# Transposed query features, sums as extra columns and no max subtraction in a gated linear-attention kernel

## Chip, cores and metric

One core of one Trainium2 chip. The metric is the device time of the core, in microseconds. A run counts as slow when it lies over 1.5% above the fastest run of the same kernel.

## The reference, cut to what matters

```python
qkv = (x @ wqkv)            # x: 2048 x 1024 bf16; 32 heads of 32
pq = einsum("bhsd,hdf->bhsf", q, w_phi);  pk = the same of k
phi_q = concat([softmax(pq), softmax(-pq)], -1)      # 64 features a head
phi_k = concat([softmax(pk), softmax(-pk)], -1)
kv = einsum("bhsf,bhsd->bhfd", phi_k, v);  z = phi_k summed over s
o  = (phi_q @ kv) / (phi_q . z + 1e-6)
a  = o @ wo
# b: x, plus a gated FFN (3584 wide) on the one row with the largest x . w_r
# out = g * a + (1 - g) * b,  g = sigmoid(x . gate_w), one value a row
```

All sums over k must be complete before the first q row can be finished. So the kernel has a K half (V, k features, kv) and a Q half (q features, numerator, wo), and the FFN of one row is spread among them as filler.

## The kernel before

The k and q features fold w_phi into wqkv first (`wkf`, `wqf`). A half tile is 128 rows by 16 heads. The softmax runs in stages that the loop spreads over several rounds, and TensorE (PE) transposes the finished q features (`eT`) before the numerator. Cuts are marked.

```python
def softmax_front(p_ps):                       # stage 0: copy of the scores
    nc.scalar.copy(out=ps_[:], in_=p_ps[:])
def softmax_mm(st, d2_pool):                   # stage 1: max, min, two subtractions
    nc.vector.tensor_reduce(out=mx[:], in_=st["ps"][:], axis=AX.X, op=ALU.max)
    nc.vector.tensor_reduce(out=mn[:], in_=st["ps"][:], axis=AX.X, op=ALU.min)
    nc.gpsimd.tensor_tensor(out=d1[:], in0=st["ps"][:], in1=_bc(mx[:], ...), op=ALU.subtract)
    # d2: the same with mn, on POOL for q, on DVE for k
def softmax_exp(st):                           # stage 2
    nc.scalar.activation(out=e[:, :, 0, :], in_=st["d1"][:], func=ACTF.Exp)
    nc.scalar.activation(out=e[:, :, 1, :], in_=st["d2"][:], func=ACTF.Exp, scale=-1.0)
def softmax_norm(st, normalize):               # stage 3: DVE sums; POOL scales
    ...
def q_s4(u):                                   # PE transposes of e, copied by ACT
    for pl in range(NPU):
        nc.tensor.transpose(out=eT_ps[:, pl, :], in_=e[...], identity=ident[:])
    nc.scalar.copy(out=eT[:], in_=eT_ps[:])
def q_s5(u):                                   # numerator (64 columns), denominator (2 columns)
    ...
def q_s6(t):                                   # PE transposes of o, copied by ACT
    ...
# weights: loaded plainly, transposed on PE; logits: 128 matmuls of 2 columns on PE
```

## Time and profile before

| | before |
|---|---|
| median | 356.94 us (356.36 to 357.41, 4 runs) |
| mean granted clock of PE | 0.992 |
| PE busy | 318.7 us, 89% of the span |
| PE idle, 40 to 220 us | 17.6 us (180 less 162.4) |

The page also divides the span into 40 slices. A digit is the busy share of a slice in tenths; `PEclk` is PE's granted clock in tenths of full speed (9 is 90% or more). This is PE in the kernel before:

```profile
PE   2998996989989899698989898999999999999982
PEclk9999999989999999999999999999999999999998
```

PE falls short of 9 in many slices up to slice 25 (223 us; the last kv matmul of the K half starts at 196.5) and is full from there to the tail.

### The profile page before, as it was taken

How to read it: one execution, taken by the hardware profiler on the slowest of the kernel's cores; microseconds unless marked ns; L12 is line 12 of the kernel's file. 1: busy time of each engine (PE TensorE's matmuls, PEld its weight loads, DVE VectorE, ACT ScalarE, POOL GpSimd, SP SyncE). 2: the span in 40 equal slices, each digit the busy share in tenths (PEclk: the TensorE clock that was granted, in tenths of full speed). 3: DMA queues.
4: the chain of work that ended last, by engine and by line, in shares of the span. 5: the costliest groups of instructions: out<-in, count | busy, mean ns of one | idle time of the engine just before them, and what ended most of it. 6: DMA issues, size and time to landing. Idle time of an engine off the chain costs nothing. (4 is left out here: it accounts for less than half of the span.)

```text
span 356.3 us, 8221 instructions
## 1 busy us (share of the span) xinstructions
PE 318.7 (89%) x3322; PEld 189.1 (53%) x3372; DVE 258.5 (73%) x455; ACT 211.8 (59%) x333; POOL 202.8 (57%) x231
## 2 busy tenths in 40 slices
PE   2998996989989899698989898999999999999982
PEld 1578552445555555354446475555555555556640
DVE  3034288877987975688887989888888888887641
ACT  1456645535556655254554679777777777778630
POOL 1000056467776763577778978687777766665101
PEclk9999999989999999999999999999999999999998
DMA  8997920028823033333336660012221111122111
GB/s 253 375 386 238 324 87 2 0 87 272 261 94 118 2 120 118 120 118 120 120 118 237 233 245 31 31 59 61 61 60 61 60 60 46 59 61 62 47 59 30
DMA packets 33894, 43.60 MB, mean 122 GB/s; under 512 B 2624, under 2 KB 23104, under 8 KB 33856
## 3 DMA queue, kind: packets, MB, share of 16 engines
q1 hardware_dynamic: 32704, 43.00, 35.5%
q8 instruction: 26, 0.43, 0.5%
q10 hardware_dynamic: 1120, 0.07, 0.2%
q14 instruction: 12, 0.10, 0.1%
q0 software_dynamic: 32, 0.00, 0.0%
HBM read 38.87 MB, written 4.20 MB: 121 GB/s over the span
## 5 line engine op out<-in xcount | busy, mean ns | idle before, releaser
L247 POOL TENSOR_TENSOR d<-pks,mx 128x512 bf16<-128x512 bf16 x64 | 67.1, 1049 | 89.1 <-DVE mx L243 82.4
L263 DVE TENSOR_REDUCE ssum<-e 128x32 f32<-128x1024 bf16 x64 | 77.4, 1211 | 33.3 <-ACT e L257 33.2
L256 ACT ACTIVATE e<-d 128x512 bf16<-128x512 bf16 x64 | 40.5, 633 | 61.7 <-POOL d L247 55.4
L269 POOL TENSOR_TENSOR phi<-e,rs 128x1024 bf16<-128x1024 bf16 x32 | 61.2, 1912 | 22.0 <-DVE rs L267 21.0
L304 PE MATMUL pk<-wkf,xT 128*128 128x512 bf16 x242 | 61.7, 385 | 4.6 <-DVE d L251 4.1
L352 PE MATMUL pq<-wqf,xT 128*128 128x512 bf16 x237 | 59.2, 379 | 3.9 <-ACT pks L235 2.0
L292 PE MATMUL pv<-wv_sb,xT 128*128 128x512 bf16 x248 | 61.1, 385 | 0.8 <-issue 0.2
L428 PE MATMUL kv_b<-wo_sb,oT 128*128 128x512 bf16 x247 | 57.1, 379 | 1.5 <-ACT oT L416 1.0
L243 DVE TENSOR_REDUCE mx<-pks 128x16 f32<-128x512 bf16 x64 | 42.4, 662 | 17.2 <-ACT pks L235 13.9
L257 ACT ACTIVATE e<-d 128x512 bf16<-128x512 bf16 x64 | 40.4, 631 | 7.6 <-POOL d L249 7.2
L374 ACT COPY eT<-eT_ps 128x1024 bf16<-128x1024 bf16 x32 | 32.6, 1019 | 17.6 <-PE eT_ps L370 17.6
L244 DVE TENSOR_REDUCE mn<-pks 128x16 f32<-128x512 bf16 x64 | 42.8, 669 | 0.0
L428 PEld LDWEIGHTS <-oT 128*128 128x128 bf16 x256 | 24.8, 98 | 30.2 <-ACT oT L416 1.1
L304 PEld LDWEIGHTS <-xT 128*128 128x128 bf16 x256 | 24.2, 98 | 30.2 <-issue 5.9
L292 PEld LDWEIGHTS <-xT 128*128 128x128 bf16 x256 | 24.1, 99 | 27.3 <-issue 3.1
L352 PEld LDWEIGHTS <-xT 128*128 128x128 bf16 x256 | 24.1, 97 | 27.0 <-issue 2.7
L277 POOL TENSOR_TENSOR e<-e,rho 128x512 bf16<-128x512 bf16 x32 | 33.6, 1051 | 2.5
L249 POOL TENSOR_TENSOR d<-pks,mn 128x512 bf16<-128x512 bf16 x32 | 33.6, 1049 | 1.4
L431 DVE SCALAR_TENSOR_TENSOR o_out<-kv_b,gate,xg 128x512 bf16<-128x512 f32 x32 | 23.8, 744 | 10.6 <-PE kv_b L428 7.9
L141 DVE COPY wT<-pTw 128x1024 bf16<-128x1024 bf16 x16 | 10.9, 683 | 19.7 <-PE pTw L139 19.7
L296 ACT CAST vaug<-pv 128x512 bf16<-128x512 f32 x32 | 18.6, 581 | 8.5 <-PE pv L292 8.4
L235 ACT CAST pks<-pk 128x512 bf16<-128x512 f32 x32 | 18.5, 578 | 5.7 <-PE pk L304 4.7
(94 smaller groups left out, 432.9 us busy)
## 6 DMA issues: line engine op xcount, KB each, us to landing
wch<-in_B_w_gate_dram SPq DMA_DIRECT2D x7, 1024.0 KB, 6.0
wch<-in_B_w_up_dram SPq DMA_DIRECT2D x7, 1024.0 KB, 5.1
wchd<-in_B_w_down_dram SPq DMA_DIRECT2D x7, 1024.0 KB, 5.2
xs_t<-in_A_x_dram SPq DMA_DIRECT2D x16, 256.0 KB, 5.5
xin<-in_A_x_dram SPq DMA_DIRECT2D x16, 256.0 KB, 2.7
out_dram<-o_out SPq DMA_DIRECT2D x32, 128.0 KB, 1.7
wv_sb<-in_A_wqkv_dram SPq DMA_DIRECT2D x2, 1024.0 KB, 5.7
wk_raw<-in_A_wqkv_dram SPq DMA_DIRECT2D x1, 2048.0 KB, 10.1
```

Of the source, the lines that this page charges most:

```text
L243: nc.vector.tensor_reduce(out=mx[:], in_=st["ps"][:], axis=AX.X, op=ALU.max)
L244: nc.vector.tensor_reduce(out=mn[:], in_=st["ps"][:], axis=AX.X, op=ALU.min)
L247: nc.gpsimd.tensor_tensor(out=d1[:], in0=st["ps"][:], in1=_bc(mx[:], [P, HH, DH]), op=ALU.subtract)
L249: nc.gpsimd.tensor_tensor(out=d2[:], in0=st["ps"][:], in1=_bc(mn[:], [P, HH, DH]), op=ALU.subtract)
L256: nc.scalar.activation(out=e[:, :, 0, :], in_=st["d1"][:], func=ACTF.Exp)
L257: nc.scalar.activation(out=e[:, :, 1, :], in_=st["d2"][:], func=ACTF.Exp, scale=-1.0)
L263: nc.vector.tensor_reduce(out=ssum[:].rearrange("p h s -> p (h s)"), in_=e[:].rearrange("p h s f -> p (h s) f"), axis=AX.X, op=ALU.add)
L269: nc.gpsimd.tensor_tensor(out=phi[:].rearrange("p h s f -> p (h s) f"), in0=e[:].rearrange("p h s f -> p (h s) f"), in1=_bc(rs[:].rearrang ...
L292: nc.tensor.matmul(pvf, lhsT=xT[:, kb, t * P:(t + 1) * P], rhs=wv_sb[:, kb, hf * 512:(hf + 1) * 512], start=(kb == 0), stop=(kb == KB - 1))
L304: nc.tensor.matmul(pkf, lhsT=xT[:, kb, t * P:(t + 1) * P], rhs=wkf[:, kb, hf * 512:(hf + 1) * 512], start=(kb == 0), stop=(kb == KB - 1))
L352: nc.tensor.matmul(pqf, lhsT=xT[:, kb, t * P:(t + 1) * P], rhs=wqf[:, kb, hf * 512:(hf + 1) * 512], start=(kb == 0), stop=(kb == KB - 1))
L428: nc.tensor.matmul(kv_b[nh][:], lhsT=oT[:, kb, :], rhs=wo_sb[:, kb, sl], start=(kb == 0), stop=(kb == KB - 1))
```

## The change

The intent is to take work off PE and POOL. Without max subtraction both exponentials come straight from PSUM. The q features are computed transposed (`wqf` is the stationary side), so the `eT` transposes go. The four softmax sums become eight extra columns of the numerator matmul. Weights and o are transposed by DMA. As exponentials without max subtraction can overflow, norms of x and of the folded weights bound the scores; a flag at the end selects a slow general path, never taken with these inputs. The core of the diff, shortened and with cuts:

```diff
-    nc.scalar.copy(out=ps_[:], in_=p_ps[:])          # and max, min, d1, d2
+    nc.scalar.activation(out=e[:, :, 0, :], in_=pk[:], func=ACTF.Exp)
+    nc.scalar.activation(out=e[:, :, 1, :], in_=pk[:], func=ACTF.Exp, scale=-1.0)
 ...
-    wrgT ...: 128 logit matmuls of 2 columns
+    for c in range(2):      # logits: row-sum products on DVE, two rows broadcast to 128 partitions
+        nc.vector.scalar_tensor_tensor(out=junk2[:], in0=xt_[:], scalar=1.0, in1=wr_bc[:, c, :],
+                                       op0=ALU.mult, op1=ALU.mult, accum_out=rg[:, c, t:t + 1])
+    nc.scalar.activation(out=junk[:], in_=xt_[:], func=ACTF.Square, accum_out=nx2[:, t:t + 1])
 ...
-    prep_j: 8 PE transposes of the weights, DVE copy, fold
+    nc.sync.dma_start_transpose(out=wT[which][:, :, kb * P:(kb + 1) * P], in_=A_wqkv[...])
+    fold: 8 matmuls, 2 DVE copies, and the norm:
+    nc.vector.scalar_tensor_tensor(out=junk3[:], in0=wf[:, kb, :], ..., accum_out=nw2[:, which, kb:kb + 1])
 ...
+def q_front(sb, j):   # q features transposed, 512 rows at a time
+    nc.tensor.matmul(pq[:], lhsT=wqf[:, kb, j * P:(j + 1) * P], rhs=xT[:, kb, sb * SB:(sb + 1) * SB], ...)
+def q_num(t, hf):
+    num = psK.tile([P, 3 * 512], F32, name="num", tag="kvn")        # one buffer of three banks
+    nc.tensor.matmul(num[:, b * NSTR:b * NSTR + KVW], lhsT=E[...], rhs=KV[:, sg, j, :], ...)   # 136 columns
+    # DVE: ds (copy of the sums), pr, den, rden, ab (two), then T = num * ab; POOL: o = T0 + T1
+def q_oT(t):
+    if t < NT - 1: nc.sync.dma_start_transpose(out=oT[:], in_=o_f)
+    else: 8 PE transposes and an ACT copy
 ...
+    nv = 12      # V halves taken as done when the K loop starts (16 are)
 ...
+    fv = nc.values_load(flag[0:1, 0:1], min_val=0, max_val=1)
+    with tc.If(fv > 0):
+        general_path(...)
```

## The prediction

> **What bounds the kernel now.** I read the page first: busy time, the 40 slices, the costliest groups. Then the windows of 20 us, then the timeline of TensorE (PE) in the last half, then the chain that ended last. The busy shares and four windows:
>
> ```profile
> PE 318.7 (89%) x3322; PEld 189.1 (53%) x3372; DVE 258.5 (73%) x455; ACT 211.8 (59%) x333; POOL 202.8 (57%) x231
> ...
> 0.00:20.00 20.00, 12.92 (x70) 7.28 (x72) 4.00 (x9) 5.66 (x7) 1.35 (x17) 1.00 0.96 322
> 60.00:80.00 20.00, 17.42 (x157) 8.57 (x159) 16.52 (x29) 8.33 (x16) 11.89 (x11) 0.94 0.12 37
> 280.00:300.00 20.00, 19.70 (x181) 11.45 (x183) 16.89 (x31) 15.31 (x22) 14.41 (x19) 1.00 0.19 65
> 340.00:357.00 17.00, 8.55 (x59) 4.09 (x57) 4.75 (x9) 2.16 (x2) 0.95 (x1) 0.91 0.14 46
> ```
>
> After start and length, a window gives PE, weight loads, DVE, ACT, POOL. From 220 to 320 us PE is full (19.7 of 20); DVE follows at 16.9. Busy PE counts overlapping latencies, so I take the cost of a matmul from start to start:
>
> ```profile
> 261.74 1.89 PE L428 MATMUL kv_b<-wo_sb,oT 128*128 128x512 bf16 x8
> 263.47 0.61 PE L370 MATMUL eT_ps<-ident,e 128*128 128x128 bf16 x8
> 263.91 0.19 PE L399 MATMUL num_ps<-kvm,eT 128*128 128x64 bf16 x1
> ...
> 264.35 0.61 PE L414 MATMUL oT_ps<-ident,o_sb 128*128 128x128 bf16 x8
> ```
>
> Eight 512-column matmuls take 263.47-261.74 = 1.73 us (0.216 each), eight 128-column transposes 0.44 (0.055), the 16 small numerator and denominator matmuls up to 264.35 another 0.44 (0.0275). In the same way the timeline gives 0.0325 for a kv matmul and 0.025 for a one-column FFN matmul. The stream of before: 1024 x 0.216 = 221.2; 768 of 128 columns x 0.055 = 42.2; 512 x 0.0275 = 14.1; kv 256 x 0.0325 = 8.3; FFN 672 x 0.025 = 16.8; logits 128 x 0.025 = 3.2. Sum 305.8 us. So 356.3 - 305.8 = 50.5 us are PE gaps: about 10 before the first V matmul, about 12 in the tail, the rest in the K half, where PE waits for the softmax that DVE, POOL and ACT hand to each other.
>
> The groups that the argument uses (busy, mean ns of one):
>
> ```profile
> L263 DVE TENSOR_REDUCE ssum<-e 128x32 f32<-128x1024 bf16 x64 | 77.4, 1211 | 33.3 <-ACT e L257 33.2
> L269 POOL TENSOR_TENSOR phi<-e,rs 128x1024 bf16<-128x1024 bf16 x32 | 61.2, 1912 | 22.0 <-DVE rs L267 21.0
> L243 DVE TENSOR_REDUCE mx<-pks 128x16 f32<-128x512 bf16 x64 | 42.4, 662 | 17.2 <-ACT pks L235 13.9
> L374 ACT COPY eT<-eT_ps 128x1024 bf16<-128x1024 bf16 x32 | 32.6, 1019 | 17.6 <-PE eT_ps L370 17.6
> L431 DVE SCALAR_TENSOR_TENSOR o_out<-kv_b,gate,xg 128x512 bf16<-128x512 f32 x32 | 23.8, 744 | 10.6 <-PE kv_b L428 7.9
> ```
>
> 512 more elements cost a DVE reduction 1211-662 = 549 ns; I use this slope for new DVE shapes.
>
> **What the Trainium skill says.** "VectorE: DVE Perf Modes", section "The perf-mode tier table": reductions, and anything with an fp32 operand in PSUM, run at one element a cycle. The trace agrees: 549 ns for 512 elements. "SBUF — State Buffer", section "Who interferes with whom": a DVE instruction with two SBUF inputs contends with a GpSimd instruction that reads SBUF, and the second is blocked whole. The change adds 48 such instructions; before has hardly any, so its trace can't show it. "DMA: Bandwidth & Descriptors", section "Latency and other measured facts": a DMA transpose with a non-contiguous middle dimension moved 261 GB/s. Before has none; its plain loads reach 375 to 386 GB/s. "Runtime: NRT & Kernel Launch", section "Instruction fetch mechanics": a taken branch to a target out of the fetched window stalls for a fetch. Before has no such branch.
>
> **The change, part by part.** On PE: the 256 transposes of e go (256 x 0.055 = -14.1), 120 of the 128 transposes of o (-6.6, now DMA), the 128 weight transposes (-7.0, now DMA), the 128 logit matmuls (-3.2, now DVE). The 256 numerator matmuls with the sums as columns have 136 columns, an estimated 0.058 each, 15.0 against 14.1 (+0.9). The order shows 288 V matmuls for 256: four halves are computed twice (32 x 0.216 = +6.9). New stream 305.8 - 23.1 = 282.7 us.
>
> POOL loses all subtractions and the rho products: phi 61.2 and 32 additions x 1.05 = 33.6, so 203 falls to about 97. ACT loses pks and eT, gains 16 squares (about 1.1 each): about 147 from 212. Both are then far from bounding.
>
> DVE loses max, min, d2 and the q sums, but gains: 32 products with row sums for logits and 16 for the norms of the folded weights, 1024 elements each, estimated 744+549 = 1.29 us, 61.9 in all; 32 PSUM copies of folded weights (about 0.67, 21.4); per half tile of q a chain of seven: five small (0.22+0.16+0.15+0.30 and a reciprocal 0.24, from small rows of the groups) and one of 1024 elements (the old o_sb of 512 took 0.68, so 0.68+0.55 = 1.23), 2.30 x 32 = 73.6. With sums and reciprocals of k (38.8+11.0), xT copies 5.5, o_out 23.8 and some 10 of rest: 246 us, against 258.5. DVE is hardly relieved, and its work moves to the start.
>
> *Start.* On DVE the copy of the first xT stands behind five of the new products, so V starts at an estimated 13.5 us (before 9.8). The x load for tile 4 stands behind eight weight transposes: 5.5 MB ahead of it, 3.5 at 380 GB/s and 2 at 261 or less, so it lands at about 22 to 26. From there to the first k sum DVE has 18 products (23.2), 16 fold copies (10.7) and 3 xT copies (2.1) = 36 us. The K loop starts at about 58 (before about 43), after some 37 us of PE stream: about 21 us of PE gap.
>
> *K loop.* PE: k 55.3, 20 V halves 34.6, kv 8.3, FFN 9.6 to 10.4, folds and xT 6.6 = 115. In its first 7 rounds DVE needs 1.55 (sum, reciprocal) + 2.58 + 0.34 = 4.5 us a round against PE 3.8: 5 to 6 us of gap. Later PE leads. Head-of-line waits on the load queue (transposes of the q weights ahead of x tiles 12 to 15): 3.
>
> *Turn to Q* (last phi, KV copies, the FFN's hidden vector): 4, partly filled by q matmuls. *Q rounds:* PE num 0.47 + q 1.73 + wo 1.73 = 3.93; DVE 0.74 + 2.30 = 3.04, so hidden; 2 of loose gaps. *Drain:* eight rounds without q have 2.2 us of PE but 3.04 of DVE: 7. *Tail:* num, chain 2.3, POOL 1.05, transposes, ACT copy 1.0, wo 3.45, o_out, then the output and the last accumulation as before:
>
> ```profile
> 346.43 3.20 PE kv_b L428 x14
> 349.65 0.76 DVE o_out L431
> 350.43 1.69 DMA out_dram<-o_out
> 352.21 0.59 issue
> ```
>
> These 6 us from o_out to the end of the span remain; I add 2 for the flag and its branch. Tail gap 12. Gaps: 21 + 6 + 3 + 4 + 2 + 7 + 12 = 55. Sum 282.7 + 55 = 338. I write 337.
>
> **Rivals.** (a) *DVE bounds the first third more than I think.* For: 246 us of DVE, 48 products that POOL's 1.9 us phi can block. Against: POOL is only half loaded. If each product in the K loop waits 1 us and the start takes 8 more, 337 becomes 350 to 358 and the gain is gone. (b) *DMA transposes are slow.* For: short runs, one queue. In a Q round, o of a tile is ready about 4.5 us after the second numerator starts, and wo of it starts at 7.86+0.47+1.73 = 10.1: a transpose may take 5.5 us from issue. Before's plain 256 KB load landed in 2.7 us, so double is still hidden; at 8 us each of 15 tiles stalls 2.5 us (+38), and the start loses 10. That would make 360 to 385. (c) *The products are cheap* (two bf16 elements a cycle, 0.7 us): DVE in the start falls by some 11 us and the K loop is PE's alone: 318 to 325. (d) *The cut softmax chain closes the K half's gaps and nothing replaces them*: near 282.7 + 35 = 318.
>
> **Range and chances.** The PE saving of 23 us is sure; the gaps may go from 50 to 35 or to 75. So 337, with 319 to 355 eight times in ten. Faster by over 2% is under 349.4: my own sum puts it 12 us inside, 0.76. Within 2% 0.15, slower than 363.7 0.09, mostly by rival (b).
>
> **What would show it.** PE busy should fall while its gaps shift to the first 60 us; matmul counts 288 V, 256 num with 136 columns and 0.058 us spacing; DVE busy near 246 with products of 1.29; POOL under 100. First k sum near 58 us; Q rounds of 3.9 to 4.0 us; DMA transposes of o under 5.5 us from issue to landing; 2 us between the last accumulation and the end that before lacks. I am wrong if DVE is busy under 215 (c), if wo waits for oT by DMA (b), or if Q rounds are over 4.3.

## The result and the profile after

The changed kernel takes 353.24 us median (352.04 to 353.82, 4 runs) against 356.94. The ratio is 0.9882, 95% interval 0.9852 to 0.9913. All ratios here are the mean time of one kernel's fast runs over that of the other's fast runs of the same rounds, so they are not quite the ratios of the quoted medians. The prediction was 337: its range held, but the gain was a fifth of the forecast.

Busy times, then PE, DVE and the clock in slices:

```profile
PE 296.9 (84%) x2478; PEld 161.0 (46%) x2518; DVE 246.1 (70%) x501; ACT 137.4 (39%) x230; POOL 115.5 (33%) x81
...
PE   1398979879779999999998999969999999847590
...
DVE  4623999999968435599994237866777777766740
...
PEclk9999999999989999999999999999999999987987
```

PE lost 21.8 us of busy time, and 4 came out at the end. DVE is full from slice 5 to slice 11 (35 to 97 us), and from slice 35 on PE is mostly at 4 to 8 tenths, with its clock down as well. Four windows, the first three as the prediction read them before:

```profile
0.00:20.00 20.00, 6.28 (x38) 4.19 (x39) 12.59 (x22) 7.69 (x11) 5.27 (x16) 1.00 0.91 239
60.00:80.00 20.00, 15.89 (x122) 8.66 (x123) 20.00 (x31) 14.89 (x26) 8.22 (x4) 1.00 0.74 158
280.00:300.00 20.00, 19.84 (x121) 10.33 (x122) 15.37 (x42) 7.72 (x12) 6.67 (x6) 1.00 0.40 99
300.00:320.00 20.00, 13.88 (x78) 6.98 (x78) 13.91 (x41) 4.53 (x5) 5.07 (x5) 0.85 0.34 86
```

Three places stand out. PE works 6.3 of the first 20 us (12.9 before). In the early K rounds DVE is busy for all 20 us and PE for 15.9. The Q rounds are full until 300 us; then come the last eight half tiles without q matmuls, the *drain*, where PE is busy 13.9 of 20 us at a clock of 0.85.

Here is PE's timeline in the drain (start, duration, line and operation, count; in brackets the idle time ahead of it and what ended it):

```profile
307.00 1.25 PE L523 MATMUL po<-wo_sb,oT 128*128 128x512 bf16 x5 [1.61 <-DMA oT<-o_sb]
308.09 0.64 PE L480 MATMUL num<-KV,E 128*128 128x136 bf16 x8
308.78 2.32 PE L523 MATMUL po<-wo_sb,oT 128*128 128x512 bf16 x10
...
311.87 0.65 PE L480 MATMUL num<-KV,E 128*128 128x136 bf16 x8 [0.62 <-DVE T L495]
316.35 0.61 PE L523 MATMUL po<-wo_sb,oT 128*128 128x512 bf16 x1 [3.83 <-DMA oT<-o_sb]
316.75 1.11 PE L480 MATMUL num<-KV,E 128*128 128x136 bf16 x8
317.66 4.38 PE L523 MATMUL po<-wo_sb,oT 128*128 128x512 bf16 x12
```

The numerator at 316.75 has to wait behind *one* wo matmul of the next tile, and that one waits 3.83 us for a DMA transpose. Its own buffer had been free since 315.33, when the product `T` of the numerator before ended; so it lost 1.4 us by standing behind that matmul. In this trace PE keeps the order in which its matmuls were laid when the kernel was built. From 317.66 twelve matmuls take 4.38 us, where 12 x 0.216 = 2.6 would do: from 316 to 320 us, around this wait, the clock is 0.50. The DVE product `T` that frees the numerator's buffer starts at 305.29, 310.59, 314.10, 319.25, 324.35, 328.45, 331.96 and 335.48, so a round takes 30.19 / 7 = 4.31 us.

At the start, these are the loads on the queue of SyncE (SP), and then what DVE does once x tile 4 has landed:

```profile
10.32 13.69 SPq L273 DMA_TRANSPOSE wT<-in_A_wqkv_dram  x8
24.19 1.90 SPq L242 DMA_DIRECT2D xs_t<-in_A_x_dram  x4
```

```profile
27.55 1.23 DVE L265 SCALAR_TENSOR_TENSOR junk<-xs_t,wr_bc 128x1024 bf16<-128x1024 bf16 x1 [7.73 <-DMA xs_t<-in_A_x_dram]
...
35.07 1.89 DVE L283 CAST wkf<-pW 128x512 bf16<-128x512 f32 x3 [4.54 <-PE pW L281]
...
64.43 1.21 DVE L409 TENSOR_REDUCE ssum<-e 128x32 f32<-128x1024 bf16 x1
```

The last line is the first k sum. DVE waits 7.73 us for x4, and then 4.54 us for the first fold of the k weights (`pW`), which stands behind V matmuls in PE's order.

In the early K rounds two engines block each other. These are the DVE timeline and then the POOL timeline, same columns:

```profile
70.04 1.16 DVE L265 SCALAR_TENSOR_TENSOR junk<-xs_t,wr_bc 128x1024 bf16<-128x1024 bf16 x1
...
71.13 2.92 DVE L265 SCALAR_TENSOR_TENSOR junk<-xs_t,wr_bc 128x1024 bf16<-128x1024 bf16 x1
...
75.11 1.21 DVE L265 SCALAR_TENSOR_TENSOR junk<-xs_t,wr_bc 128x1024 bf16<-128x1024 bf16 x1
```

```profile
70.27 2.70 POOL L413 TENSOR_TENSOR phi<-e,rs 128x1024 bf16<-128x1024 bf16 x1 [0.38 <-DVE rs L411]
```

The product takes 1.21 us alone and 2.92 beside phi, and phi takes 2.70 instead of 1.91. This bears out the Trainium skill, "SBUF — State Buffer", section "Who interferes with whom", by which a DVE instruction with two SBUF inputs contends with a GpSimd instruction that reads SBUF, and whoever comes first blocks the other: phi starts while the product of 70.04 runs and ends at 73.0, 1.9 us after that product; the product of 71.13 ends at 74.05, 1.1 us after phi. The pattern repeats every second round (DVE: 2.91 us at 80.67, 2.92 at 90.22), and the rounds alternate between 3.6 and 5.9 us.

### The profile page after: what moved, and what is told of

The parts are those of the page before. It is cut to its first block, busy times and chain, and to the rows that moved or that the text cites. A ratio compares the mean times of both kernels' runs of the same rounds, so it can differ in the third digit from the quotient of the medians.

```text
span 352.0 us, 6368 instructions
## 1 busy us (share of the span) xinstructions
PE 296.9 (84%) x2478; PEld 161.0 (46%) x2518; DVE 246.1 (70%) x501; ACT 137.4 (39%) x230; POOL 115.5 (33%) x81
## 5 line engine op out<-in xcount | busy, mean ns | idle before, releaser
L499 POOL TENSOR_TENSOR o_sb<-T 128x512 bf16<-128x512 f32 x32 | 40.6, 1267 | 108.2 <-DVE T L495 108.2
L523 PE MATMUL po<-wo_sb,oT 128*128 128x512 bf16 x249 | 63.0, 394 | 10.7 <-DMA oT<-o_sb 10.3
L459 PE MATMUL pq<-xT,wqf 128*128 128x512 bf16 x244 | 59.8, 379 | 0.9 <-ACT E L462 0.3
L265 DVE SCALAR_TENSOR_TENSOR junk<-xs_t,wr_bc 128x1024 bf16<-128x1024 bf16 x32 | 42.8, 1364 | 13.6 <-DMA xs_t<-in_A_x_dram 13.6
L409 DVE TENSOR_REDUCE ssum<-e 128x32 f32<-128x1024 bf16 x32 | 38.7, 1208 | 17.1 <-ACT e L406 17.1
L495 DVE TENSOR_TENSOR T<-num,ab 128x1024 f32<-128x1024 f32 x32 | 39.2, 1225 | 3.5 <-DVE ab L493 0.5
L393 ACT CAST v_all<-pv 128x512 bf16<-128x512 f32 x36 | 21.2, 588 | 47.5 <-PE pv L391 47.5
L391 PEld LDWEIGHTS <-xT 128*128 128x128 bf16 x288 | 27.0, 100 | 27.9 <-issue 2.2
L525 DVE SCALAR_TENSOR_TENSOR o_out<-po,gate,xg 128x512 bf16<-128x512 f32 x32 | 23.8, 745 | 22.0 <-PE po L523 22.0
L402 PEld LDWEIGHTS <-xT 128*128 128x128 bf16 x256 | 24.1, 98 | 26.5 <-issue 1.3
L459 PEld LDWEIGHTS <-wqf 128*128 128x128 bf16 x256 | 23.5, 97 | 23.5 <-issue 0.6
```

Of the source, the lines that this page charges most:

```text
L265: nc.vector.scalar_tensor_tensor(out=junk2[:], in0=xt_[:], scalar=1.0, in1=wr_bc[:, c, :], op0=ALU.mult, op1=ALU.mult, accum_out=rg[:, c, ...
L391: nc.tensor.matmul(pvf, lhsT=xT[:, kb, t * P:(t + 1) * P], rhs=wv_sb[:, kb, hf * 512:(hf + 1) * 512], start=(kb == 0), stop=(kb == KB - 1))
L393: nc.scalar.copy(out=v_all[:, t * 2 + hf, :, 0:DH], in_=pv[:])
L402: nc.tensor.matmul(pkf, lhsT=xT[:, kb, t * P:(t + 1) * P], rhs=wkf[:, kb, hf * 512:(hf + 1) * 512], start=(kb == 0), stop=(kb == KB - 1))
L409: nc.vector.tensor_reduce(out=ssum[:], in_=e2, axis=AX.X, op=ALU.add)
L459: nc.tensor.matmul(pq[:], lhsT=wqf[:, kb, j * P:(j + 1) * P], rhs=xT[:, kb, sb * SB:(sb + 1) * SB], start=(kb == 0), stop=(kb == KB - 1))
```

## The experiments

Fourteen kernels ran (no e10 is on record), each with five rounds against the kernel before; all gave correct results. One execution of the kernel before, in the rounds of e14 and e15, took 636 us; it counts as slow and is left out. The last column is the ratio less 0.9882 (the changed kernel), times 357 us: the effect against the changed kernel. Each ratio's interval is about ±0.4%, so differences below some 2 us are not told apart. A trace is one execution, and not always one near the median (e6: 350.0, e7: 341.8), so lengths of rounds come with that spread.

| run | edit to the changed kernel | median us | ratio to before | effect us |
|---|---|---|---|---|
| e1_logits_pe | logits back on PE | 345.83 | 0.9647 | -8.4 |
| e2_oT_pe_drain | o of tiles 11 to 14 transposed on PE | 350.12 | 0.9794 | -3.1 |
| e3_no_branch | no flag read, no conditional | 349.95 | 0.9817 | -2.3 |
| e4_no_dup | V computed once | 347.71 | 0.9751 | -4.7 |
| e5_no_norms | no norms | 348.68 | 0.9748 | -4.8 |
| e6_two_num | second numerator buffer in the drain | 347.56 | 0.9706 | -6.3 |
| e7_two_num_oT_pe | e6 and e2 | 345.13 | 0.9674 | -7.4 |
| e8_wr_late | broadcast loads later | 352.84 | 0.9863 | -0.7 |
| e9_x_first | x4 to x7 ahead of the transposing loads | 351.96 | 0.9832 | -1.8 |
| e13_warm | filler matmuls in the drain | 346.54 | 0.9690 | -6.9 |
| e15_order | PE in program order in the drain | 347.96 | 0.9710 | -6.1 |
| e11_combined | e4, e7, e9, norms of k moved | 332.70 | 0.9298 | -20.8 |
| e14_combined_logits_pe | e11 and logits on PE | 335.92 | 0.9387 | -17.7 |
| e12_before_no_max | *kernel before*, without max subtraction | 339.76 | 0.9500 | -13.6 |

### The start and the early K rounds

**e1_logits_pe.** Logits on PE as in the kernel before.

```diff
-        for c in range(2):      # 32 products with row sums on DVE, and the two broadcast loads
-            nc.vector.scalar_tensor_tensor(out=junk2[:], in0=xt_[:], ..., accum_out=rg[:, c, t:t + 1])
+        for t in range(NT):     # in gates_and_route, once all tiles are there
+            for kb in range(KB):
+                nc.tensor.matmul(lg_ps[:, t, :], lhsT=xT[:, kb, t * P:(t + 1) * P], rhs=wrgT[:, kb:16:8], ...)
```

> The changed kernel with the logits back on TensorE (128 two-column matmuls, the 32 row-sum products on DVE and the two 256 KB broadcast loads gone). Theory 'DVE bounds the first third': the first k sum comes at about 50 us instead of 64.4, the early K rounds fall from 4.8 to about 3.9 us, TensorE pays 3.2 us for the 128 matmuls; total 334 to 342 us. Rival 'DVE there is only busy beside something else that bounds': first k sum stays over 60 us or the K loop gives it back, total 350 to 356 us.

Measured: 345.83 us, between the two. The profiled run counts as slow (348.7), so what follows is seen once and explains no part of the ratio, which rests on fast runs. The first k sum starts at 56.4 us (64.4 in the changed kernel) and the last kv matmul at 184.5 (190.0). So the products, with their loads, did hold the start, by 8 us. But the K loop from the first sum to the last kv grew from 125.5 to 128.1 us in this trace. The clock is a likely part of that. In the kernel before, the scheduler had spread these 128 small matmuls from 25.8 to 52.9 us; here they come in one block, from 80.95 to 84.4 us, and the clock falls at its end. Windows of 2 us around the block (after start and length: PE, weight loads, DVE, ACT, POOL, clock):

```profile
82.00:84.00 2.00, 2.00 (x81) 2.00 (x79) 0.77 (x2) 0.07 (x1) 0.96 (x1) 0.89 0.00 0
84.00:86.00 2.00, 2.00 (x24) 0.77 (x22) 0.69 (x4) 0.18 (x1) 0.95 (x1) 0.50 0.00 0
86.00:88.00 2.00, 2.00 (x6) 0.67 (x6) 0.21 (x1) 0.13 (x1) 0.00 (x0) 0.50 0.05 10
```

PE counts as busy all the time, and yet from about 84 to 90 us it runs at half clock. The dip of the kernel before at 78 us likewise follows a block of 64 one-column FFN matmuls, but there PE had also been idle (busy 1.47 and 1.16 of 2 us in the windows from 72 to 76), so that it does not separate the two.

**e5_no_norms.** The 16 norm products and the 16 squares removed, sums set to zero (right for these inputs only).

```diff
-        nc.scalar.activation(out=junk[:], in_=xt_[:], func=ACTF.Square, accum_out=nx2[:, t:t + 1])
-        nc.vector.scalar_tensor_tensor(out=junk3[:], in0=wf[:, kb, :], ..., accum_out=nw2[:, which, kb:kb + 1])
```

> The changed kernel without the norms for the range test (16 row-sum products of the folded weights on DVE and 16 squares on ACT gone, the sums set to zero; right for these inputs only). Eight of the products, 8 x 1.3 = 10 us of DVE, stand before the first k sum. Theory 'DVE bounds the start': the first k sum comes 7 to 10 us earlier than 64.4 and the total falls to 343 to 347 us. Rival 'loads and TensorE take the bound over at once': under 3 us gained, 350 to 353 us.

Measured: 348.68 us, between the two; first k sum at 60.7. Only 3.7 of the 10 us of removed DVE work came out there: in this trace DVE waits 1.44 us for an x tile shortly before that sum. The run also removes ACT's squares, so it does not price the DVE products alone.

**e8_wr_late.** The broadcast loads behind the V weights.

```diff
-        nc.scalar.dma_start(out=wr_bc[:, 0, :], in_=B_w_r.unsqueeze(0).to_broadcast([P, D]))   # and gate_w
+    nc.sync.dma_start(out=wr_bc[:, 0, :], in_=B_w_r...)      # behind the second half of wv
```

> The changed kernel with the two broadcast loads of the router and gate rows (256 KB each as written) issued behind the V weights on the load queue, instead of at the very start on ACT's. Theory 'they delay x0 and x1': x1 lands near 8 us instead of 11.6 and V starts 2 to 4 us earlier; the products then come later, so of this 0 to 3 us reach the end: 350 to 353 us. Rival 'DVE alone sets the start': first k sum at 64 us or later, 353 to 356 us.

Measured: 352.84 us, no difference. PE's timeline of this run shows why:

```profile
8.27 2.08 PE L256 MATMUL pT<-ident,xs_t 128*128 128x128 bf16 x16 [3.73 <-DMA xs_t<-in_A_x_dram]
10.14 0.63 PE L391 MATMUL pv<-wv_sb,xT 128*128 128x512 bf16 x1
...
26.54 1.04 PE L256 MATMUL pT<-ident,xs_t 128*128 128x128 bf16 x8 [5.24 <-DMA xs_t<-in_A_x_dram]
```

x1 lands at 8.3 us and V starts at 10.1 instead of 17.5, as the theory said. But PE then waits for x4, and the folds start at 33.5 (34.7 in the changed kernel). While x4 is late, the late V start costs next to nothing (folds 1.1 us earlier, first k sum at 63.3 instead of 64.4).

**e9_x_first.** x4 to x7 queued ahead of the eight transposing loads.

```diff
-    for kb in range(KB):
-        wT_load(0, kb)
     ... xT_tile(0..3), k_v(0..3, 0), xload(4..7)
+    for kb in range(KB):
+        wT_load(0, kb)
```

> The changed kernel with the loads of x tiles 4 to 7 queued ahead of the eight transposing loads of the k weights, not behind them. Theory 'x4 behind the transposes (27.5 us) starts the long DVE queue late, while DVE idles from 20 to 34 us': x4 lands before 20 us, the first k sum comes at 54 to 59 us instead of 64.4, total 343 to 348 us. Rival 'the transposes then wait as long for the slots of x0 to x3, and the folds start later': first k sum at 62 us or later, total 351 to 355 us.

Measured: 351.96 us, the rival's range; first k sum at 62.0. PE no longer waits for x4, but V starts at 17.0, so the folds begin at 32.2. Each of e8 and e9 removes one of two limits of about equal length. Both together on the changed kernel alone were not run. e14 below has both, V once, and no logit products; its V starts at 10.0, and yet its folds begin at 34.7. There PE waits 2.85 us (to 31.58) for ACT to copy V out of PSUM, while ACT had stood 4.01 us before a square, for the norm of an x tile that had not landed. e11 shows the same (2.50 and 3.65 us). So ACT's squares are a third limit of the start, which no run removes from those two kernels.

**e4_no_dup.** V computed once.

```diff
-    nv = 12
+    nv = 16
```

> The changed kernel with the four halves of V that are computed twice computed once (32 matmuls of 512 columns fewer, 6.9 us of TensorE stream). Theory 'they lie in the early K rounds, which DVE bounds': total 351 to 353.5 us, the early K rounds stay near 4.8 us. Rival 'TensorE bounds there': 346 to 347 us.

Measured: 347.71 us, 4.7 of the 6.9 us. My theory, that the duplicates hide in rounds that DVE bounds, mostly falls. The early rounds did stay at 4.8 us: the eighth k sum comes at 99.0 us (98.5 before the edit). The gain comes later, where PE is full: the last kv matmul at 185.8 instead of 190.0. A plausible reading, not tested: with fewer V halves left at 99 us, less work remains for the stage that PE bounds.

### The drain

**e2_oT_pe_drain.** PE transposes and an ACT copy for tiles 11 to 14.

```diff
-        if t < NT - 1:
+        if t < 11:
             nc.sync.dma_start_transpose(out=oT[:], in_=o_f)
```

> The changed kernel with o of the tiles 11 to 14 transposed on TensorE and copied by ACT (as tile 15 is), instead of by DMA. Theory 'in the drain TensorE, in order, waits for the DMA transposes (1.6 + 3.8 + 1.8 + 0.2 us) before it can start the next numerator': rounds from 4.3 us to about 3.5, total 346 to 349 us. Rival 'the loop through the single numerator buffer (3.5 us and more) bounds the drain whatever the transposes do': total 351 to 354 us.

Measured: 350.12 us, between the two; rounds fall from 4.31 to 3.78 us.

**e6_two_num and e7_two_num_oT_pe.** Odd half tiles of the drain put their numerator into two PSUM banks that the q matmuls no longer need, and the sums into a third; e7 adds e2.

```diff
+        if t * 2 + hf >= 24 and hf == 1:
+            nA = [psA.tile([P, 512], F32, name="numA", tag="pA") for _ in range(2)]
+            # 128 columns of KV into nA[sg], the 8 sum columns into small_ps; T in two halves
```

> The changed kernel, where in the drain (half tiles 25, 27, 29, 31) the numerator goes to two PSUM banks that the q matmuls have left free, with its sums in a third, so that the numerator has a second buffer; o is still transposed by DMA. If TensorE's wait in its order for the DMA transposes is the larger cost, the rounds stay near 4 us: total 349 to 352 us. If the single numerator buffer is the larger cost: rounds near 3.2 us, total 344 to 347 us.

> Both together: second numerator buffer in the drain, and o of tiles 11 to 14 transposed on TensorE. Theory 'the drain costs what the two waits cost, and without both DVE sets its rounds': rounds of 3.0 to 3.3 us instead of 4.3, total 343 to 346 us. Rival 'the drain is bound by something else (DVE with small operations, the half clock of TensorE)': as with the transposes alone, 349 to 351 us.

Measured: 347.56 and 345.13 us. The starts of `T` give rounds of 3.68 us for e6 and 3.01 for e7. So with both waits gone the drain runs at the 3.04 us that the prediction had reckoned from DVE alone, and DVE is indeed the full engine there (20.05 of 21 us):

```profile
303.00:324.00 21.00, 18.75 (x174) 11.26 (x173) 20.05 (x61) 7.34 (x7) 8.88 (x7) 1.00 0.16 53
```

By the ratios e6 and e7 are 1.1 us apart, which is not told apart; only the rounds of the two traces tell them.

**e13_warm.** Four matmuls of 512 columns that nobody reads, behind each numerator of the drain.

```diff
+        if t * 2 + hf >= 24:
+            for kb in range(4):
+                nc.tensor.matmul(dm[:], lhsT=wqf[:, kb, 0:P], rhs=xT[:, kb, 0:512], ...)
```

> The changed kernel with four matmuls of 512 columns, whose result nobody reads, behind each numerator of the drain (+0.9 us of TensorE a round, in time in which it waits for DVE). Theory 'the half clock that TensorE gets after its waits (0.5 from 314 to 320.5 and from 334.5 to 338 us) lengthens the drain': clock 1.00 in the drain, total 349 to 351.5 us. Rival 'the rounds are set by the loop through the numerator buffer and by the DMA transposes': total 353 to 356 us.

Measured: 346.54 us, 2.5 us below the range of the theory. That was suspicious. In its trace the rounds are 3.52 us and no wo matmul waits for a DMA transpose, although the transposes were not touched. The filler had also changed the order in which the scheduler laid PE's work: an even numerator, eight of wo, numerator, eight of wo, instead of wo matmuls of the next tile ahead of a numerator. Two causes at once, so one more run:

**e15_order.** No filler; numerators and wo of the drain are pinned to the order of the program.

```diff
-                nc.tensor.matmul(num[...], ...)
+                mm = nc.tensor.matmul(num[...], ...)
+                if t * 2 + hf >= 24: tc.keep_in_program_order(mm)      # the same for wo
```

> The changed kernel with one thing altered: in the drain TensorE's matmuls keep the order in which the program writes them (numerator, eight of wo, numerator, eight of wo), where the scheduler had put one to five matmuls of the next wo, which wait for a DMA transpose, ahead of the next numerator. No filler matmuls, DMA transposes as before. Theory 'TensorE's order puts the transposes on the path of the numerators': rounds of 3.5 us as in the run with filler matmuls, total 345 to 348 us. Rival 'the filler helped by keeping the clock full': rounds of 4 us and more with half clock in the drain, total 350 to 353 us.

Measured: 347.96 us. PE's timeline in this drain:

```profile
310.96 0.65 PE L480 MATMUL num<-KV,E 128*128 128x136 bf16 x8 [1.15 <-DVE T L497]
311.45 1.89 PE L525 MATMUL po<-wo_sb,oT 128*128 128x512 bf16 x8
314.48 0.65 PE L480 MATMUL num<-KV,E 128*128 128x136 bf16 x8 [1.14 <-DVE T L497]
315.39 1.90 PE L525 MATMUL po<-wo_sb,oT 128*128 128x512 bf16 x8 [0.26 <-DMA oT<-o_sb]
318.00 0.65 PE L480 MATMUL num<-KV,E 128*128 128x136 bf16 x8 [0.71 <-DVE T L497]
```

All seven rounds take 3.52 us, and every numerator now waits for `T`, the reader of its only buffer. The clock in the drain is 1.00 without any filler: the half clock came with PE's waits and went with them. So e13's filler was not needed, and its order was the cause; how much of the 6.1 us went by way of the half clock is not separated. From 4.31 to 3.52 us a round is the order. That the rest, down to the 3.01 of e7, is the single buffer is argued from these waits: no run has the pinned order and the second buffer, as e7 also transposes on PE. The two costs overlap, since the second buffer alone (e6) already gives 3.68.

**e3_no_branch.** No flag read, no conditional (right for these inputs only).

```diff
-    fv = nc.values_load(flag[0:1, 0:1], min_val=0, max_val=1)
-    with tc.If(fv > 0):
-        general_path(...)
```

> The changed kernel without reading the flag and without the conditional and its general path (right for these inputs only). The flag and branch at the end cost about 1.6 us by the trace: expected 351 to 352 us, the part from the start of the last o_out to the end 6.7 us as before instead of 8.3. Rival: the end waits for the output transfers anyway, 353 us.

Measured: 349.95 us. From the start of the last o_out to the end it takes 6.7 us (344.36 to 351.1), against 8.3 in the changed kernel (343.72 to 352.0): 1.5 us in the trace, 2.3 by the ratio, which agree within the interval.

### One part alone, and all that helped

**e12_before_no_max.** The kernel before without max, min, subtractions and copy; `e`, now written as soon as the scores are there, has 8 buffers instead of 3. Like the changed kernel without its flag it is right only while scores stay small.

```diff
-        nc.scalar.copy(out=ps_[:], in_=p_ps[:])          # and softmax_mm, softmax_exp emptied
+        nc.scalar.activation(out=e[:, :, 0, :], in_=p_ps[:], func=ACTF.Exp)
+        nc.scalar.activation(out=e[:, :, 1, :], in_=p_ps[:], func=ACTF.Exp, scale=-1.0)   # e: 8 buffers
```

> The kernel before with one part of the change alone: no max and min, no subtractions, no copy of the scores; ACT takes both exponentials straight from PSUM. From 40 to 220 us the kernel before has 17.6 us of TensorE idle time, in its windows. Theory 'the long softmax chain makes these gaps': 8 to 14 us of them close and the Q half, full already, stays: 343 to 349 us. Rival 'the gaps come from loads, routing and PSUM buffers': 353 to 358 us.

Measured: 339.76 us, better than the theory. One window from 40 to 220 us, first of the kernel before, then of e12:

```profile
40.00:220.00 180.00, 162.40 (x1739) 92.43 (x1767) 141.82 (x245) 99.60 (x180) 121.20 (x116) 0.99 0.39 131
```

```profile
40.00:220.00 180.00, 175.89 (x1898) 101.21 (x1928) 94.37 (x154) 90.63 (x156) 80.60 (x79) 1.00 0.42 136
```

PE's idle time falls from 17.6 to 4.1 us; the two traces differ by 17.2 us, and most of what remains is PE busy time, 318.7 to 315.2 us in the whole span. This one part gains 17.9 us by the ratio; the whole change gains 4.2. So the rest of the change, though it took 23 us off PE's stream in the prediction's sum, makes the kernel 13.6 us slower than this part alone. The comparison is not quite fair: e12 has no safeguard against overflow, and on the changed kernel the norms (e5) and the flag (e3) were worth 4.8 + 2.3 = 7.1 us. With that price, an estimate and not a run, e12 would still gain some 10.7 us.

**e11_combined.** Edits e4, e7 and e9, and the norm products of the k weights moved from the folds to rounds 12 to 19 of the K loop, where DVE is half idle. Flag and general path stay, so it keeps the changed kernel's safeguard.

> All that helped, together and right for all inputs: x4 to x7 ahead of the transposes, the norm products of the k weights moved out of the start into rounds 12 to 19 of the K loop, V computed once, second numerator buffer and TensorE transposes in the drain. If the costs add (start 8 to 12, V 4.7, drain 7.4, from 353.2): 330 to 335 us. If TensorE or the loads take over as the bound of the first third: 338 to 344 us.

Measured: 332.70 us (331.79 to 336.68), 7% under the kernel before and the fastest of all. Its rounds in the drain are 3.0 us, its first k sum comes at 60.3 us and its last kv at 180.4. The costs add: e4, e7, e9 and, for the moved norms, e5 sum to 18.7 us; e11 has 20.8. (e5 is a generous price for that: it removed all norms, and e11 only moves half of the products.)

**e14_combined_logits_pe.** e11 with each tile's logits on PE right behind its transposes.

> The combined kernel (332.7 us), with the logits of each tile on TensorE right behind the tile's transposes (128 two-column matmuls, 3.2 us), so that the 32 products and the two broadcast loads are gone as well. Theory 'DVE still bounds its start and early rounds': first k sum near 50 us instead of 60.3, total 322 to 327 us. Rival 'TensorE bounds once DVE is relieved, and pays for the logits': 331 to 336 us.

Measured: 335.92 us, in the rival's range and 3 us slower than e11. In its windows from 40 to 60 us PE is busy 9.97 and 10.00 of 10 us and DVE 5.7 and 3.2, as the rival has it. But then the first k sum comes at 62.6, later than e11's 60.3, although PE starts the matmuls of the second half tile of scores at 58.0. The ACT timeline and the DVE timeline show why:

```profile
60.41 1.06 ACT L273 ACTIVATE junk<-xs_t 128x1024 bf16<-128x1024 bf16 x1 [3.75 <-DMA xs_t<-in_A_x_dram]
...
61.94 0.59 ACT L413 ACTIVATE e<-pk 128x512 bf16<-128x512 f32 x1
```

```profile
62.56 1.22 DVE L416 TENSOR_REDUCE ssum<-e 128x32 f32<-128x1024 bf16 x1 [8.05 <-ACT e L413]
```

ACT stands 3.75 us before a square, for the norm of an x tile that is still on its way, and takes the exponentials only after it. PE in turn waits 3.39 us for ACT's copy of xT and then runs at half clock from 64 to 68 us. So the price of the logits on PE and this wait are mixed in the 3 us: in this arrangement DVE is the better place for the logits, but that PE's time is the reason is not shown.

## Why the prediction was wrong

**Right.** The stream: 288 V matmuls, numerators spaced (303.50 - 303.02) / 8 = 0.060 us, PE 21.8 us less busy. Unblocked products 1.22 us against 1.29. Q rounds 3.92 us against 3.93. DMA transposes of o 3.1 us from issue to landing against a limit of 5.5. Flag and branch together 1.5 to 2.3 us against 2; whether any of it is a fetch is not shown.

**Right by luck.** From x4's landing to the first k sum 36.9 us against 36: DVE is busy only 32.2 of them, because its products and copies follow each other faster than reckoned, and 4.5 us are the wait for the first fold, which the sum did not have. Early K rounds 4.8 us against 4.5: without the 1.7 us that phi blocks DVE in every second round they would be some 3.9, an estimate from the timeline above; so rival (a)'s blocking was real, and the work was smaller. DVE 246.1 us in all against 246 holds such blocked time too: the 32 logit products have a mean of 1.36 us.

**Near.** POOL 115.5 us against under 100, because phi (2.15 us mean) and the addition (1.27) are slower than reckoned, phi where DVE's products contend with it.

**Wrong: the start.** The step was "it lands at about 22 to 26 us", and from it "The K loop starts at about 58". x4 landed at 27.5 and the first k sum came at 64.4: 6.4 us late. I had priced the eight transposing loads by their bytes; what counted is that they hold the queue's engine for 13.7 us (10.3 to 24.0), and the x loads stand behind them. But x4 is not the whole cause: with it moved ahead (e9), the first k sum came only 2.4 us earlier, because the folds then wait for V. What DVE does between folds and first k sum is what can be won there (e1, e5).

**Wrong: the drain.** This is the step that failed: "eight rounds without q have 2.2 us of PE but 3.04 of DVE: 7." I took the larger of two busy sums as the length of a round. Measured are 4.31 us; over the seven intervals of `T` that is 7 x 1.27 = 8.9 us. The round is a loop of latency: numerator, six small DVE operations, `T`, and only then the next numerator, because `num` has one buffer. That makes 3.52 us (e15). Then PE's fixed order put wo matmuls ahead of numerators, and so put the DMA transposes on the path (6.1 us in all, e15). I had shown those transposes to be hidden with the slack of a round *with* q matmuls, and the drain has none.

The two misses are 6.4 + 8.9 = 15.3 of the 16 us; smaller ones, either way, nearly cancel. The 6.9 us of duplicate V were in the sum and were real (e4). None of my rivals named the drain; (a) had nearly the right number for another reason. The sign that I had named for (b), "if wo waits for oT by DMA", did appear (10.3 us in all), but not because the transposes are slow: none of those of o took over 3.7 us to land. In rival (d) I wrote that the shorter chain would close the K half's gaps "and nothing replaces them". e12 shows the first half true, 13.5 us of gaps; the changed kernel fills the place with DVE products at the start and waits in the drain. I had priced the whole change but never its simplest part by itself.

Left open: how much of the start is the loads, how much V and how much ACT's squares, as e8 and e9 were not run together on the changed kernel; how the loss in the drain divides between the order and the half clock; and why 4.7 of 6.9 us of duplicate V came out.

## What to carry to other kernels

Price every stage by its dependency loop and by the number of its buffers, not by the larger of two busy sums: pipeline slack that holds in the steady state is gone in the drain. Where an engine works in order, as PE did here, look at which instructions the scheduler has laid ahead of the critical one; pinning two kinds of matmul to the program's order was worth 6 us here. Try the simplest part of a large change alone before adding the rest: one part, though without the safeguard, was worth four times the whole.

## What the Trainium skill lacked or had wrong

- "TensorE: Matmul & The Clock Gate", section "Part 1: The HAM clock gate (the "warmup" mystery)": it gives an idle window of about 3.4 us for the fall to half clock. Half clock around long waits is borne out, that length is not: in the changed kernel the clock is 0.53 from 314 to 316 us, when PE had been idle since 312.5, and 0.50 from 336 to 338 us, after a wait of 2.87 us. The section does not say that a block of two-column matmuls can let the clock fall too: 0.50 from 84 to 90 us in e1, with PE counted as busy throughout (one trace, of a slow run).
- "DMA: Bandwidth & Descriptors", section "Latency and other measured facts": its 261 GB/s for DMA transposes was not reached; from 10.3 to 24.0 us, with eight of 256 KB and plain loads in flight, the DMA engines were full (share 1.06) and moved 234 GB/s in all. The figure says nothing of the queue: such an instruction held its issuing engine 1.24 us and more, a plain load mostly 0.3 to 0.5.
